# Twelve equal groups of 256 tokens, scans on full row tiles, and one listed order of jobs for all engines

## The chip, the cores and the metric

The kernel runs on one core of a Trainium2 chip. Time is device time in microseconds (us): the median of 3 runs is 389.97 us (389.54 to 390.4). The core's engines each work through their own queue in order: TensorE (PE) multiplies matrices, ScalarE (ACT) and VectorE (DVE) work element by element, GpSimd (POOL) too, and SyncE (SP) issues most transfers (DMAs). They wait for each other through semaphores.

## The reference

The input is a gated linear attention with 4 batches, 8 heads, 768 tokens and 48 features per head, followed by a channel mix.

```python
for t in range(S):
    state = alpha[:, :, t, :, None] * state + np.einsum('bhd,bhe->bhde', k[:, :, t], v[:, :, t])
    y[:, :, t] = np.einsum('bhd,bhde->bhe', q[:, :, t], state)
# x is y with the heads side by side: 384 features per token; x_prev is x one token earlier
xk = mu_k * x + (1.0 - mu_k) * x_prev
xr = mu_r * x + (1.0 - mu_r) * x_prev
k = np.maximum(xk @ w_k, 0.0)          # 384 -> 1024
v = k * k @ w_v                        # 1024 -> 384
r = 1.0 / (1.0 + np.exp(-(xr @ w_r)))  # 384 -> 384
return (r * v).astype(np.float32)
```

## The kernel before

The 768 tokens of a batch are cut into chunks of 128, and the chunks into groups: three groups of two chunks in batch 0, two groups of three chunks in each other batch, nine groups in all. The head's features lie on the partitions, two heads in one tile of 112 rows (48, a hole of 16, 48), so four such tiles (layers, `p` in the code) hold the eight heads.

Attention of a group. VectorE runs two scans per layer: a forward scan gives the running product of alpha (`pp`, line 258), a backward scan the product from a token to the group's end (`al`, line 281). q is multiplied by the one and k by the other (lines 276 and 284, on VectorE or GpSimd by the tables `QG` and `QH`). Per chunk, TensorE transposes k (`trans`, line 336, copied out by ScalarE into `ht`), and `visit` makes the state's growth (line 399), the scores (line 346), and, for the chunk before, the output from masked scores (line 365) and from the state (line 383). VectorE masks the scores (`am`, line 352), adds up the state (`st`, lines 411 and 415) and, at a group's end, rescales it (line 417). The output leaves as features on partitions (`xt`, lines 425 and 431); 16 rows of the fourth head pair's tile are moved by transfers inside SBUF into the holes of the other three (line 439), so that the channel mix sees three full tiles of 128 features.

Channel mix of a group. `mix` makes xk and xr: ScalarE scales (line 478), VectorE adds the shifted tokens (line 479); then a high part in fp32r (line 482) and the rest (line 483). `moe` multiplies high by high, low by high and high by low: `up` (line 500) 72 matmuls with the group's tokens as columns, the squares of the relu (lines 508 to 514, `kh` and `kl`), the gate (line 525) and `down` (line 540) with 384 columns. The weights come as 64-bit floats and are split into a high and a low part on the chip (`split`, lines 208 to 222), in pieces of 768 columns.

What sets the order. TensorE's and SyncE's queues follow the program text: `merge` deals the attention of group g+1 between the matmuls of group g by weights (`LEAD`, `PAD`), and in the first group `FILL` says after which of its units the weight pieces and the scans of the next groups are written. The other engines' queues are put in order by the framework's scheduler.

Of the kernel before, what the change touches and what calls it, by code (L numbers as in the profile page):

```python
# [35 lines left out]
NT = 3  # L36
NF = FF // 128
START = 2.0**30
# [4 lines left out]
LEAD = 12.0  # L43
LEAD0 = 8.0
PAD = 3.0
ENG = {
    "wk": ("AP", "AD", "AP", "AP"),
    "wr": ("DP", "DP"),
    "wv": ("DP", "DP", "AD", "DP"),
}  # L50
K2 = "AAD"
QH = ("DDDD", "PDPD", "PPPP")
QG = ("PDDD", "DPDP", "DDDP")
FILL = [
# [3 lines left out]
]  # L58
FIRST_LOADS = ["k", "wk0", "al", "wk1", "q", "wk2", "wk3", "v"]
WARM = 22  # L60
HOLD = 14
NX = HB - D

# [5 lines left out]
def merge(main, side, lead):  # L69
    total = max(sum(w for w, _ in main) - lead, 1.0)  # L70
    load = sum(w for w, _ in side)
    done = spent = 0.0
    side = list(side)
    for w, f in main:
        f()
        done += w
        while side and spent / load <= done / total:
            ws, fs = side.pop(0)
            fs()
            spent += ws  # L80
    for _, fs in side:
        fs()


@with_exitstack
def gated_attention_channel_mix(
    ctx: ExitStack,
    tc: tile.TileContext,
    al_p: bass.AP,
    q_p: bass.AP,  # L90
    k_p: bass.AP,
    v_p: bass.AP,
    mu_p: bass.AP,
    wk_p: bass.AP,
    wv_p: bass.AP,
    wr_p: bass.AP,
    q_raw: bass.AP,
    k_raw: bass.AP,
    v_raw: bass.AP,
    al_raw: bass.AP,  # L100
    out: bass.AP,
):
    nc = tc.nc
    PE, ACT, DVE, POOL = nc.tensor, nc.scalar, nc.vector, nc.gpsimd

    cp = ctx.enter_context(tc.tile_pool(name="cp", bufs=1))
    p1 = ctx.enter_context(tc.tile_pool(name="p1", bufs=1))
    p2 = ctx.enter_context(tc.tile_pool(name="p2", bufs=2))
    p3 = ctx.enter_context(tc.tile_pool(name="p3", bufs=3))
    ps = ctx.enter_context(tc.tile_pool(name="ps", bufs=1, space=PSUM))  # L110
    pm = ctx.enter_context(tc.tile_pool(name="pm", bufs=3, space=PSUM))
    dp = ctx.enter_context(tc.tile_pool(name="dp", bufs=1, space=DRAM))

    zero = cp.tile([R, R], F32, name="zero")
# [705 lines left out]
```

## Time and profile before

| | us |
|---|---|
| median of 3 runs | 389.97 |
| profiled execution, span from first to last instruction | 390.1 |
| TensorE busy | 332.0 (85%) |
| VectorE busy | 281.6 (72%) |
| ScalarE busy | 188.7 (48%) |
| GpSimd busy | 65.3 (17%) |

The profile comes from one execution; its own time is the span, with nothing to add around it that the page shows. Busy times are unions of an engine's instructions. Matmuls overlap in a pipeline, so how fast they follow each other is read from their starts, not from the length of one. PEclk is the granted share of TensorE's full clock.

### The profile page before, as it was taken

The numbers are of one execution on the slowest core, as the hardware profiler recorded it, in microseconds if no ns is written. First come the engines' busy times: TensorE is split into PE (matmuls) and PEld (weight loads), VectorE is DVE, ScalarE is ACT, GpSimd is POOL, SyncE is SP. The second block draws the span as 40 slices with busy tenths as digits, with TensorE's granted clock in tenths as the row PEclk, the third lists the DMA queues.
The fourth block names the chain that finished last, engine by engine and source line by source line (L and its number), as shares of the span: only waits on it lengthen the run. The fifth ranks groups of instructions, "written<-read, shape, count | busy, mean of one in ns | idle before, by whom it ended". The sixth has DMA issues, their size and how long they took to land.

```text
span 390.1 us, 10751 instructions
## 1 busy us (share of the span) xinstructions
PE 332.0 (85%) x4590; PEld 315.5 (81%) x4590; DVE 281.6 (72%) x513; ACT 188.7 (48%) x393; POOL 65.3 (17%) x84
## 2 busy tenths in 40 slices
PE   7542787709995997899979997999999999999993
PEld 6432687709984996799969997999999999999993
DVE  5787989998389639988596959678965476456510
ACT  3356693236563345544355525562754555455500
POOL 5143544550021003203010220003000000000000
PEclk9655769968999799999999998999999999999998
DMA  8978455830703070305510341025100110011001
GB/s 212 273 249 293 136 152 143 233 91 24 212 25 92 12 214 22 91 3 172 142 42 2 100 144 42 3 74 169 44 2 2 37 43 3 3 37 40 0 23 47
DMA packets 15958, 35.56 MB, mean 91 GB/s; under 512 B 1600, under 2 KB 9568, under 8 KB 15904
## 3 DMA queue, kind: packets, MB, share of 16 engines
q1 hardware_dynamic: 14736, 33.72, 29.2%
q10 hardware_dynamic: 1168, 1.09, 1.1%
q8 instruction: 38, 0.62, 0.7%
q14 instruction: 16, 0.13, 0.1%
HBM read 28.90 MB, written 4.72 MB: 86 GB/s over the span
## 4 chain that ended last, share of the span: by engine, by line
PE 47%; DVE 20%; DMA 6%; issue 4%; ACT 3%; ACTq 0%; DVEq 0%
PE pk L500 19%; PE pv L540 13%; PE pg L525 5%; DVE al L281 4%; DMA xt<-xt 4%; DVE pp L258 4%; DVE x L479 3%; PE yu L365 2%; DMA q<-q_p 2%; DVE xkl L483 2%; DVE q L276 1%; PE pt L336 1%; DVE kl L514 1%; PE sp L346 1%; PE yu L399 1%
## 5 line engine op out<-in xcount | busy, mean ns | idle before, releaser
L500 PE MATMUL pk<-xkh,wkh 128*128 128x384 f32 (+1 forms) x216 | 51.4, 345 | 21.7 <-ACT xkh L482 21.7
L540 PE MATMUL pv<-wvh,kl 128*128 128x384 f32 x192 | 64.9, 338 | 2.4 <-DVE kl L514 2.4
L540 PE MATMUL pv<-wvl,kh 128*128 128x384 f32 x192 | 64.7, 337 | 0.0
L540 PE MATMUL pv<-wvh,kh 128*128 128x384 f32 x192 | 64.4, 335 | 0.0
L500 PEld LDWEIGHTS pk<-xkh,wkh 128*128 128x128 f32 x216 | 37.9, 203 | 24.5 <-ACT xkh L482 23.6
L508 ACT ACTIVATE r<-pk 128x384 f32<-128x384 f32 (+1 forms) x72 | 32.3, 454 | 41.2 <-PE pk L500 38.4
L500 PE MATMUL pk<-xkh,wkl 128*128 128x384 f32 (+1 forms) x216 | 49.6, 340 | 0.0
L500 PE MATMUL pk<-xkl,wkh 128*128 128x384 f32 (+1 forms) x216 | 48.6, 335 | 0.1
L284 POOL TENSOR_TENSOR k<-k,al 112x768 f32<-112x768 f32 (+1 forms) x18 | 31.1, 1733 | 91.3 <-DVE al L281 50.0
L512 DVE TENSOR_TENSOR k<-r 128x384 f32<-128x384 f32 (+1 forms) x56 | 30.0, 535 | 22.7 <-ACT r L508 22.1
L478 ACT ACTIVATE x<-xt,mu 128x384 f32<-128x384 f32 (+1 forms) x54 | 28.5, 575 | 35.6 <-DMA xt<-xt 25.5
L514 DVE TENSOR_TENSOR kl<-k,kh 128x384 fp32r<-128x384 f32 (+1 forms) x72 | 36.7, 509 | 11.0 <-ACT kh L513 5.8
L281 DVE TENSOR_TENSOR_SCAN al<-al 112x383 f32<-112x383 f32 (+1 forms) x36 | 39.7, 1137 | 1.3 <-ACT junk L265 1.1
L500 PEld LDWEIGHTS pk<-xkl,wkh 128*128 128x128 f32 x216 | 38.4, 203 | 0.8 <-DVE xkl L483 0.3
L540 PEld LDWEIGHTS pv<-wvh,kl 128*128 128x128 f32 x192 | 36.1, 188 | 3.4 <-DVE kl L514 3.4
L500 PEld LDWEIGHTS pk<-xkh,wkl 128*128 128x128 f32 x216 | 37.2, 202 | 0.9
L258 DVE TENSOR_TENSOR_SCAN pp<-al,tiny 112x384 f32<-112x384 f32 (+1 forms) x36 | 33.9, 963 | 4.2 <-DMA al<-al_p 4.2
L540 PEld LDWEIGHTS pv<-wvl,kh 128*128 128x128 f32 x192 | 36.0, 188 | 0.0
L540 PEld LDWEIGHTS pv<-wvh,kh 128*128 128x128 f32 x192 | 36.0, 188 | 0.0
L513 ACT ACTIVATE kh<-r 128x384 fp32r<-128x384 f32 (+1 forms) x72 | 34.7, 488 | 1.4
L479 DVE SCALAR_TENSOR_TENSOR x<-xt,nu,x 128x384 f32<-128x384 f32 (+1 forms) x54 | 31.9, 631 | 2.7 <-ACT x L478 2.7
L425 ACT COPY xt<-yu 112x512 f32<-112x512 f32 x24 | 14.1, 588 | 35.8 <-DVE st L415 25.3
(149 smaller groups left out, 531.3 us busy)
## 6 DMA issues: line engine op xcount, KB each, us to landing
out<-sig SPq DMA_DIRECT2D x24, 192.0 KB, 1.9
al<-al_p SPq DMA_DIRECT2D x6, 672.0 KB, 5.3
k<-k_p SPq DMA_DIRECT2D x6, 672.0 KB, 4.7
q<-q_p SPq DMA_DIRECT2D x6, 672.0 KB, 7.4
v<-v_p SPq DMA_DIRECT2D x6, 600.0 KB, 4.2
wkraw<-wk_p SPq DMA_DIRECT2D x4, 768.0 KB, 14.6
vraw<-wv_p SPq DMA_DIRECT2D x4, 768.0 KB, 5.5
v<-v_p SPq DMA_DIRECT2D x3, 400.0 KB, 6.6
```

What stands on the lines that cost most here:

```text
L258: DVE.tensor_tensor_scan(pp[:, p], al[:, p, :n], tiny[:R].to_broadcast([R, n]), initial=START, op0=ALU.mult, op1=ALU.max,)
L281: DVE.tensor_tensor_scan(back, back, back, initial=al[:, i, n : n + 1], op0=ALU.mult, op1=ALU.bypass)
L284: (DVE if QH[min(g, 2)][p] == "D" else POOL).tensor_tensor(k[:, hp], k[:, hp], al[:, hp, 1:], op=ALU.mult)
L478: ACT.activation(x, xt[:, t, 1 : 1 + n], AF.Copy, scale=mu[:, i, t : t + 1])
L479: DVE.scalar_tensor_tensor(x, xt[:, t, 0:n], nu[:, i, t : t + 1], x, op0=ALU.mult, op1=ALU.add)
L500: PE.matmul(pk, w[:, t, cols], x[:, t], start=part == 0 and t == 0, stop=part == 2 and t == NT - 1,)
L508: ACT.activation(r, pk, AF.Relu)
L512: DVE.tensor_tensor(k2, r, r, op=ALU.mult)
L513: ACT.activation(kh[:, f], r, AF.Square)
L514: DVE.tensor_tensor(kl[:, f], k2, kh[:, f].bitcast(F32), op=ALU.subtract)
L525: PE.matmul(pg, x[:, i, cols], w[:, i], start=part == 0 and i == 0, stop=part == 2 and i == NT - 1,)
L540: PE.matmul(pv, x[:, f, cols], w[:, f], start=f == 0 and i == 0, stop=f == NF - 1 and i == 2,)
```

## The change

The kernel is rewritten. What it computes stays the same, and so do the formulas on each engine.

- Groups: all groups of the channel mix have two chunks (`N` = 256 tokens, twelve pairs `m`). The scans work on the same pairs, only the first pair is cut into two groups of one chunk.
- Row tiles: from the second pair on, the fourth layer's features are laid by the host into the holes of the other three, so scans and products work on three tiles of 128 rows. After the products, transfers inside SBUF copy the 16-row pieces into a fourth layer (`gather`, two for k and two for q in each of eleven groups), since the attention matmuls still read 48 rows per head.
- Feature tiles paired: `up` handles two blocks of 128 hidden features at once into one PSUM bank, so relu, squares and residue work on 512 columns per instruction; the high and low parts of xk and xr are made for all three tiles at once (768 columns).
- Order: every job has a name (`sf` forward scan, `sb` backward scan, `qp` and `kp` products, `gq` and `gk` gathers, `tr` transposes, `vi` visit, `mk` mask, `ad` state addition, `cx` cross addition, `mv` feature transfer, `sx` and `sy` scale and shift, `xh` and `xl` high and low part, `up`, `re`, `s2`, `sh`, `sl` the squares, `ga` gate, `dn` down, `ml` and `so` the output). `ORDER` lists all of them once, for all engines; a suffix puts a job on another engine (`:P` GpSimd, `:D` VectorE, `:A` ScalarE's DMA queue), and `#` followed by a number stands for so many dummy matmuls. `plan` only derives which jobs a job needs.
- Inputs and weights lie in DRAM as whole pieces with a contiguous run per partition; k's loads carry the empty fourth layer along.

```diff
-CUTS = [[2, 2, 2], [3, 3], [3, 3], [3, 3]]
-GROUPS = [(b, sum(cut[:i]), n) for b, cut in enumerate(CUTS) for i, n in enumerate(cut)]
+CB = S // C
+NC = B * CB
+SIZES = [[1, 1, 2, 2], [2, 2, 2], [2, 2, 2], [2, 2, 2]]
+GROUPS = [(b, sum(z[:i]), n) for b, z in enumerate(SIZES) for i, n in enumerate(z)]
 NG = len(GROUPS)
-GMAX = 3 * C
+GROUP_OF = [g for g, (_, _, n) in enumerate(GROUPS) for _ in range(n)]
...
-K2 = "AAD"
-QH = ("DDDD", "PDPD", "PPPP")
-QG = ("PDDD", "DPDP", "DDDP")
...
+PAIRED = (0,)
+LAYERS = [NP if m in PAIRED else H * D // 128 for m in HOME]
+ROWS = [R if n == NP else 128 for n in LAYERS]
+CUTS = [[slice(0, 2), slice(2, 4)] if n == NP else [slice(0, 3)] for n in LAYERS]
...
+ORDER = """
+bc.0 Lal.0 Lqq.0 Lkk.0 Lqq.1 Lal.1 Lal.2 Lvv.0 Lvv.1 jk.0.0 sf.0.0 Lkk.1 sf.0.1 Lk1 jk.0.1 sf.0.2 Lk0 rc.0.0
+sf.0.3 Lk3 sb.0.1 Lr1 qp.0.1:P qp.0.0 Lk2 rc.0.1 sb.0.0 Lqq.2 ends.0 sb.0.2 Lr0 jk.1.1 kp.0.0:P sb.0.3 Lkk.2
...
-def merge(main, side, lead):
-    total = max(sum(w for w, _ in main) - lead, 1.0)
-    load = sum(w for w, _ in side)
-    done = spent = 0.0
-    side = list(side)
-    for w, f in main:
-        f()
-        done += w
-        while side and spent / load <= done / total:
-            ws, fs = side.pop(0)
-            fs()
-            spent += ws
-    for _, fs in side:
-        fs()
...
+    def scan(g):
+        n = LAYERS[g]
+        al, kk, qq, pp = (of(x, g, n) for x in ("al", "kk", "qq", "pp"))
+        end = [f"{x}e" for x in qq]
...
+        if n < NP:
+            for j in range(2):
+                add(f"gk.{g}.{j}", "SP", lambda j=j: k.gather(g, "kk", j), kk, [*of("kk", g)[n:]] if j else [f"kk.{HOME[g]}/{SUB[g]}x"])
+                add(f"gq.{g}.{j}", "SP", lambda j=j: k.gather(g, "qq", j), qq + end, [*of("qq", g)[n:]] if j else [f"qq.{HOME[g]}/{SUB[g]}x"])
...
+    def two(self):
+        return self.POOL if self.alt == "P" else self.DVE
...
+    def forward(self, g, p):
+        n = self.group(g)[1]
+        self.DVE.tensor_tensor_scan(
+            self.get("pp", g)[:, p], self.get("al", g)[:, p, :n], self.tiny[: ROWS[g]].to_broadcast([ROWS[g], n]),
+            initial=START, op0=ALU.mult, op1=ALU.max,
+        )
...
+    def k_times(self, g, two):
+        x = self.get("kk", g)[:, two]
+        self.two.tensor_tensor(x, x, self.get("al", g)[:, two, 1:], op=ALU.mult)
+
+    def q_times(self, g, two):
+        n = self.group(g)[1]
+        x = self.get("qq", g)[:, two, :n]
+        self.two.tensor_tensor(x, x, self.get("pp", g)[:, two], op=ALU.mult)
...
+    def gather(self, g, x, j):
+        m = LAYERS[g]
+        t = self.get(x, g)
+        self.queue.dma_start(t[j * HB : j * HB + D, m], t[j * HB + D : (j + 1) * HB, :m])
...
+    def x_low(self, m, i):
+        xs = self.live[f"{('xk', 'xr')[i]}.{m}"]
+        self.two.tensor_tensor(xs[:, 1], self.live[f"x.{m}.{i}"], xs[:, 0].bitcast(F32), op=ALU.subtract)
+
+    def up(self, m, f):
+        pk = self.new(f"pk.{m}.{f}", self.slots[f"pk.{m}.{f}"], [128, 2, N], space=self.ps)
+        x = self.live[f"xk.{m}"]
+        for i in range(2):
+            for w, z in ((self.hi, 0), (self.lo, 0), (self.hi, 1)):
+                for t in range(NT):
+                    at = f * PC + t * 2 * C + i * C
+                    self.PE.matmul(
+                        pk[:, i], w["k"][:, at : at + C], x[:, z, t],
+                        start=w is self.hi and z == 0 and t == 0, stop=z == 1 and t == NT - 1,
+                    )
...
+    def square(self, m, f):
+        r = self.live[f"r.{m}.{f}"]
+        k2 = self.new(f"k2.{m}.{f}", "k2", [128, 2, N])
+        if self.alt == "D":
+            self.DVE.tensor_tensor(k2, r, r, op=ALU.mult)
+        else:
+            self.ACT.activation(k2, r, AF.Square)
...
+    def square_low(self, m, f):
+        name, j, _ = self.halves(m, f)
+        x = self.live[name][:, :, 2 * j : 2 * j + 2]
+        self.two.tensor_tensor(x[:, 1], self.live[f"k2.{m}.{f}"], x[:, 0].bitcast(F32), op=ALU.subtract)
...
+    jobs, k.slots = plan(k)
+    done = set()
+    with tc.manual_schedule():
+        k.setup()
+        for name in ORDER.split():
+            if name[0] == "#":
+                k.hot(int(name[1:]))
+                continue
+            name, _, k.alt = name.partition(":")
+            _, fn, needs = jobs[name]
+            assert needs <= done, name
+            fn()
+            done.add(name)
```

GpSimd's queue behind the first group's products and until the weights of the gate. Before (`wkl`, `wrl` low parts of weights, `q`, `k` of the second group):

```order
L222 TENSOR_TENSOR wkl<-wkraw_169,wkh 128x3x256
L289 COPY pbeg<-pp_164 112x4
L290 COPY pend<-pp_164 112x4
L292 TENSOR_SCALAR pscl<-pp_164 112x4
L276 TENSOR_TENSOR q_166<-q_166,pp_164 112x256 x2
L222 TENSOR_TENSOR wkl<-wkraw_174,wkh 128x3x256 x2
L330 COPY xt_439<-xt_209 128x3
L222 TENSOR_TENSOR wrl<-rraw_384,wrh 128x768
L284 TENSOR_TENSOR k_165<-k_165,al_163 112x256
L222 TENSOR_TENSOR wrl<-rraw_386,wrh 128x384
L284 TENSOR_TENSOR k_165<-k_165,al_163 112x256
L222 TENSOR_TENSOR wvl<-vraw_388,wvh 128x768
```

and now (`kk`, `qq` of the third and fourth group):

```order
L533 TENSOR_TENSOR wkl<-raw_k_166,wkh 128x768
L581 COPY pbeg<-pp_281 128x3
L582 COPY pend<-pp_281 128x3
L585 MEMSET qq_181 32x1
L586 TENSOR_SCALAR qq_181<-pp_281 128x3
L574 TENSOR_TENSOR qq_181<-qq_181,pp_281 128x3x256
L533 TENSOR_TENSOR wkl<-raw_k_170,wkh 128x768
L569 TENSOR_TENSOR kk_193<-kk_193,al_150 128x768
L533 TENSOR_TENSOR wkl<-raw_k_177,wkh 128x768
```

The whole products of three layers now stand in this queue between the weight subtractions, where before there were products of one layer.

VectorE's queue where the second pair's features are mixed. Before (`al`, `pp` are scans, `x`, `xkl`, `xrl` the mixed features):

```order
L281 SCALAR_TENSOR_TENSOR al_937<-al_937 112x383 x4
L545 TENSOR_TENSOR sig<-pv,sig 128x384
L276 TENSOR_TENSOR q_940<-q_940,pp_938 112x768
L479 SCALAR_TENSOR_TENSOR x<-xt_439,nu,x 128x256 x2
L276 TENSOR_TENSOR q_940<-q_940,pp_938 112x768
L483 TENSOR_TENSOR xkl<-x,xkh 128x256 x2
L258 SCALAR_TENSOR_TENSOR pp_1366<-al_1365,tiny 112x384
L479 SCALAR_TENSOR_TENSOR x<-xt_439,nu,x 128x256 x2
L545 TENSOR_TENSOR sig<-pv,sig 128x384
L483 TENSOR_TENSOR xkl<-x,xkh 128x256
L483 TENSOR_TENSOR xrl<-x,xrh 128x256
L258 SCALAR_TENSOR_TENSOR pp_1366<-al_1365,tiny 112x384 x2
```

and now (`xk` is the pair of high and low part, `al_502` the alphas of the sixth group):

```order
L757 SCALAR_TENSOR_TENSOR x_0_1047<-xt_698,nu,x_0_1047 128x256 x3
L407 CAST xk_1125<-x_0_1047 128x768
L768 TENSOR_TENSOR xk_1125<-x_0_1047,xk_1125 128x768
L840 TENSOR_TENSOR sig_0_772<-pv_0_815,sig_0_772 128x384
L757 SCALAR_TENSOR_TENSOR x_1_1121<-xt_698,nu,x_1_1121 128x256 x3
L685 TENSOR_TENSOR am_1167<-sp_1055,mask 128x512
L733 TENSOR_TENSOR xt_1025<-xt_1025,sp_1055 112x2x64 x2
L699 TENSOR_TENSOR st_112<-st_116,yu_1056 112x192
L563 SCALAR_TENSOR_TENSOR al_502<-al_502 128x255
L699 TENSOR_TENSOR st_113<-st_112,yu_1056 112x192
L563 SCALAR_TENSOR_TENSOR al_502<-al_502 128x255
```

Where six features stood one by one with their subtractions and whole scans of 384 columns between them, three shifts, one cast and one subtraction of 768 columns follow each other, with short state additions and scans of 255 columns behind.

## Rows read from the trace of the kernel before

**Rows 1.** Busy times by stage; the first line names the columns, times in us.

```profile
core 0: us, PE busy (x) PEld busy (x) DVE busy (x) ACT busy (x) POOL busy (x), PEclk, DMA share, GB/s
0.00:37.60 37.60, 18.02 (x310) 15.67 (x310) 26.77 (x47) 16.78 (x27) 15.30 (x36) 0.67 0.87 258
37.60:88.26 50.66, 32.77 (x403) 30.58 (x404) 49.60 (x76) 25.90 (x61) 24.24 (x20) 0.80 0.53 152
88.26:129.40 41.14, 36.11 (x609) 34.03 (x608) 31.12 (x61) 21.97 (x57) 5.30 (x8) 0.91 0.30 84
129.40:165.00 35.60, 31.33 (x418) 29.40 (x418) 26.44 (x51) 18.91 (x42) 5.78 (x4) 0.97 0.33 92
165.00:203.50 38.50, 35.52 (x533) 33.71 (x533) 31.78 (x59) 18.02 (x37) 5.57 (x7) 1.00 0.32 91
...
278.60:316.50 37.90, 37.90 (x569) 36.52 (x568) 24.37 (x51) 19.98 (x39) 0.19 (x1) 1.00 0.06 21
```

**Rows 2.** Chain of waits, its end: start us, duration us, engine, tile, line.

```profile
353.93 12.48 PE pk L500 x72
...
367.06 4.36 PE pg L525 x24
...
383.99 0.56 DVE sig L545
```

**Rows 3.** TensorE's timeline, first main matmuls of one pair: start us, us.

```profile
98.29 0.50 PE L500 MATMUL pk<-xkl,wkh 128*128 128x256 f32 x3
...
99.31 0.50 PE L500 MATMUL pk<-xkl,wkh 128*128 128x256 f32 x3
```

**Rows 4.** VectorE's timeline outside GpSimd's longer work: start us, us.

```profile
4.19 1.27 DVE L258 TENSOR_TENSOR_SCAN pp<-al,tiny 112x256 f32<-112x256 f32 x2 [4.19 <-DMA al<-al_p]
...
10.07 0.75 DVE L281 TENSOR_TENSOR_SCAN al<-al 112x255 f32<-112x255 f32 x1
...
16.18 0.69 DVE L352 TENSOR_TENSOR am<-sp_-1_218,mask 128x512 f32<-128x512 f32 x1 [0.21 <-PE sp_-1_218 L346]
...
24.81 0.47 DVE L431 TENSOR_TENSOR xt<-xt,sp 112x128 f32<-112x128 f32 x2
25.26 0.96 DVE L222 TENSOR_TENSOR wkl<-wkraw,wkh 128x768 fp32r<-128x768 f32 x1
26.13 0.76 DVE L276 TENSOR_TENSOR q<-q,pp 112x256 f32<-112x256 f32 x2
...
36.00 0.89 DVE L479 SCALAR_TENSOR_TENSOR x<-xt,nu,x 128x256 f32<-128x256 f32 x2 [0.18 <-ACT x L478]
...
50.12 0.55 DVE L221 CAST wvh<-vraw 128x768 fp32r<-128x768 f32 x1
...
64.83 0.34 DVE L417 TENSOR_TENSOR st<-st,pscl 112x192 f32<-112x192 f32 x1
```

**Rows 5.** Timelines of VectorE and GpSimd, three places where both work.

```profile
17.65 4.09 DVE L258 TENSOR_TENSOR_SCAN pp<-al,tiny 112x256 f32<-112x256 f32 x4
18.77 1.85 POOL L222 TENSOR_TENSOR wkl<-wkraw,wkh 128x768 fp32r<-128x768 f32 x1 [7.76 <-ACT wkh L219]
...
22.48 2.40 POOL L276 TENSOR_TENSOR q<-q,pp 112x256 f32<-112x256 f32 x2
22.62 0.80 DVE L417 TENSOR_TENSOR st<-st,pscl 112x192 f32<-112x192 f32 x1
...
179.81 4.07 DVE L281 TENSOR_TENSOR_SCAN al<-al 112x383 f32<-112x383 f32 x3
180.96 2.11 POOL L284 TENSOR_TENSOR k<-k,al 112x768 f32<-112x768 f32 x1 [13.60 <-DVE al L281]
```

**Rows 6.** Transfers of the features inside SBUF, and ScalarE's longest wait for one.

```profile
xt<-xt ACTq DMA_DIRECT2D x12, 72.0 KB, 3.7
xt<-xt ACTq DMA_DIRECT2D x4, 48.0 KB, 4.6
...
ACT x L478 <- DMA xt<-xt: 8.1, 1, 8.1
```

More of the change, by code (lines that the diff above doesn't have):

```diff
@@ new lines, with __init__, place, add @@
+class Plan:
+    def __init__(self):
+        self.jobs = {}
+        self.at = {}
+        self.last = {}
+        self.since = {}
+        self.held = {}
+        self.users = {}
+    def place(self, name, slot):
+        before = self.held.get(slot)
+        self.held[slot] = name
+        self.at[name] = (slot, before)
+        self.users[name] = []
+    def add(self, name, engine, fn, reads=(), writes=()):
+        needs = set()
+        for x in (*reads, *writes):
+            if x in self.last:
+                needs.add(self.last[x])
+            t = x.split("/")[0]
+            if t in self.users:
+                self.users[t].append(name)
+                if self.at[t][1]:
+                    needs.update(self.users[self.at[t][1]])
+        for x in writes:
+            needs.update(self.since.get(x, ()))
+            self.last[x] = name
+            self.since[x] = []
+        for x in reads:
+            self.since.setdefault(x, []).append(name)
+        needs.discard(name)
+        self.jobs[name] = (engine, fn, needs)
@@ L383, in inter @@
+        if fresh:
+            for p in range(NP):
+                for s, j in quads:
+                    rr = slice(j * HB, j * HB + D)
+                    t0 = ci * C + s * HC
                     PE.matmul(
[L384 to L389 removed]
@@ new lines, in rescale, with features, leave @@
+    def rescale(self, c):
+        g = GROUP_OF[c]
+        n = self.group(g)[1]
+        x = self.by_pair(self.before(c + 1, 0))
+        self.DVE.tensor_tensor(
+            x, x, self.get("qq", g)[:R, :, n : n + 1].to_broadcast([R, NP, D]), op=ALU.mult
+        )
+    def features(self, m):
+        name = f"xt.{m}"
+        return self.live[name] if name in self.live else self.new(name, f"xt{m % 2}", [128, NT + 1, 1 + N])
+    def leave(self, c):
+        m, h = divmod(c, CM)
+        x = self.features(m)[:R, :, 1 + h * C : 1 + (h + 1) * C]
+        self.ACT.copy(
+            x.rearrange("r i (s t) -> r i s t", s=2),
+            self.stale[c][1][:R, :, : NP * HC].rearrange("r s (i t) -> r i s t", i=NP),
+        )
@@ new lines, in gate @@
+    def gate(self, m, t):
+        pg = self.new(f"pg.{m}.{t}", self.slots[f"pg.{m}.{t}"], [128, DM], space=self.ps)
+        x = self.live[f"xr.{m}"]
+        cols = slice(t * C, (t + 1) * C)
+        for z, w in ((0, self.hi), (0, self.lo), (1, self.hi)):
+            for i in range(NT):
+                self.PE.matmul(
+                    pg, x[:, z, i, cols], w["r"][:, i * DM : (i + 1) * DM],
+                    start=z == 0 and w is self.hi and i == 0, stop=z == 1 and i == NT - 1,
+                )
@@ L577, in judge @@
-        DVE.tensor_copy(flag, pf)
-    def rows(g):
-        b, c0, _, _ = span(g)
-        at = b * S + c0 * C
-        return lambda t: out[at + t * 128 : at + (t + 1) * 128, :]
-    with tc.manual_schedule(engines={mybir.EngineType.SP}):
-        first = load(1)
-        for x in FIRST_LOADS:
-            if x[0] == "w":
-                load_wk(int(x[2]))
-            else:
-                first[x]()
-    nc.scalar.dma_start(mu, mu_p)
-    nu = cp.tile([128, 2, NT], F32, name="nu")
-    POOL.tensor_scalar(nu, mu, -1.0, 1.0, op0=ALU.mult, op1=ALU.add)
@@ new lines, in sequential @@
+                rows = self.out.rearrange("(b s) e -> b s e", b=B)
+                for t in range(CM):
+                    self.gate(m, t)
+                    self.sigmoid(m, t)
+                    for h in range(2):
+                        self.down(m, t, h)
+                    self.gated(m, t)
+                    nc.sync.dma_start(
+                        rows[ds(b, 1), m * N + t * C : m * N + (t + 1) * C, :].rearrange("o s e -> (o s) e"),
+                        self.live[f"sig.{m}.{t}"],
+                    )
```

1242 lines of the change are left out of this document (673 added, 569 removed), and 3 rows, old and new, of the table FILL.

## Prediction

> **What bounds the kernel now.** I first read the busy times by stage: the stretches are cut where a group's main matmuls begin [rows 1]. In the stretch from 278.60 us TensorE is busy for all of its 37.90 us at full clock: here only the amount of matmul work counts. In the two stretches before 88.26 us it is busy for 50.8 of 88.3 us at a granted clock of 0.67 and 0.80, while VectorE is busy for 49.60 of the 50.66 us of the second: VectorE sets the pace there. Between 88.26 and 203.50 us TensorE is idle for 5.03 + 4.27 + 2.98 = 12.3 us though VectorE is not full: waits, not amount of work.
>
> How much matmul work there is I take from the end of the chain of waits, where nothing interrupts it [rows 2]: 72 matmuls with 384 columns take 12.48 us (173.5 ns each), the same for both 72-matmul stages of a group, 24 gate matmuls 4.36 us (182 ns). With 256 columns nine start within 1.02 us (113 ns each) [rows 3]. So a group of three chunks (a chunk is 128 tokens) costs 12.48 + 27 x 0.182 + 12.48 = 29.9 us, and a pair of chunks 72 x 0.113 + 18 x 0.182 + 48 x 0.1735 = 19.8 us. The full stretch of 37.90 us holds one group of three and three chunks of attention: (37.90 - 29.9)/3 = 2.67 us per chunk. The kernel before has 6 x 29.9 + 3 x 19.8 + 24 x 2.67 = 303 us of such work in a span of 390.1 us. The tail, from the last gated product on, is 390.1 - 384.0 = 6.1 us [rows 2]. The other 81 us are lost to waits and to the low clock, some 57 of them before 88.26 us. The span and the median of the runs (389.97) agree, so the sum is made on the span.
>
> **The change part by part.**
>
> Matmul work: twelve pairs cost 12 x 19.8 + 24 x 2.67 = 301 us, so the regrouping is worth 2 us, no more. The one visit that is split in two and 24 dummy matmuls stand in front of the first main matmul, where TensorE waits for VectorE anyway.
>
> VectorE, until the second pair's first matmul. In the new order the instructions ahead of it are countable. Prices are rows outside GpSimd's work, each less the 0.09 us by which a VectorE row overlaps its successor (0.96 shown, next start after 0.87) [rows 4]. 12 forward scans of 256 columns at 0.635 and 8 of 128 at 0.36 (estimate: half and a little): 10.5 us. 10 backward scans at 0.67 and 8 short ones at 0.40: 9.9. 10 joins and 3 subtractions of 768-column weight pieces (one half as long) at 0.87: 10.9. 7 casts at 0.47: 3.3. 6 masks at 0.61: 3.7. 5 pairs of cross additions at 0.45: 2.3. 9 token shifts at 0.40: 3.6. 3 feature subtractions at 0.87: 2.6. Two products of 256 columns at 0.34, a square and a gated product: 1.8. 22 short ones (state additions, reciprocals, rescales) at the 0.34 of a rescale, since they mostly wait for each other: 7.5. Sum 56 us. From there to the first matmul of the fourth pair: 9 and 11 more scans (13.1), 15 shifts (6.0), 5 masks, 5 cross additions, 15 short ones (10.4), 3 products of 768 (2.6), 3 subtractions and casts (1.8), 8 squares, residues and gated products (4.3), another 38 us, so 94 in all. The three full row tiles take a quarter of the scans away from every group but the first two: 66 scans of 256 columns and 16 of 128 stand where 72 were, 48 of them with 384 columns.
>
> What VectorE waits for itself. Its first scan waits 4.19 us for a load [rows 4]; in the first stretch it is idle for 37.60 - 26.77 = 10.8 us in all [rows 1]. The new first tile is as large, 0.23 MB, and the scans of the next group now stand ahead of the first state addition, so I keep 4.2 and put the other waits at 5: 9.2 us.
>
> GpSimd. The order hands it more: up to the second pair's first matmul 7 weight subtractions (1.85 each, one half), 6 products of three layers (2.0), 6 small ones (1.0), 4 residues of 512 columns (1.4, between those sizes) and the small copies: 41 us; up to the fourth pair's 61 us, and 116 in the whole kernel, where the kernel before shows 15.30 + 24.24 until 88.26 us and little later [rows 1]. This work is not free, because VectorE slows while it runs [rows 5]. Four forward scans took 4.09 instead of 2.54 us beside a subtraction of 1.85: 0.84 us lost per us of GpSimd. Three backward scans took 4.07 instead of 2.76 beside a product of 2.11: 0.62. A rescale took 0.80 instead of 0.34 beside products of 2.40: 0.19. The mean is 0.55; I take 0.5, and 0.19 and 0.84 as bounds.
>
> The Trainium skill, SBUF — State Buffer, section "Who interferes with whom", says that a VectorE instruction with two SBUF inputs and a GpSimd instruction that reads SBUF exclude each other, and that the later one stands still for the whole of the other. By that rule a us of GpSimd beside a queue of scans and subtractions costs VectorE up to a us; the rows show less than that in all three places. What the kernel would take by the rule is the fourth rival below.
>
> So the second pair starts at 9.2 + 56 + 0.5 x 41 = 86 us. TensorE has 34 us of work between the two pairs' first matmuls in about 45 us; at the granted 0.80 of that stretch this is 43 us, it just fits. What is left then is 301 - 19.8 - 7 x 2.67 - 0.6 (one transpose) = 262 us, for chunks 0 to 6 have been through attention: if all of it is dense, the end is at 86 + 262 + 6.1 = 354 us. If VectorE sets the pace until the fourth pair, that one starts at 9.2 + 94 + 0.5 x 61 = 134 us, and with 222.5 us left (two pairs, the third's first stage, one gate and eleven chunks are done) the end is 362 us. The order puts about 10 us of VectorE work between the fourth pair's features and their first matmul, so VectorE can lag by that much unseen: the truth lies between, and I take the middle, 358 us. Behind the fourth pair VectorE has some 116 us of work for 222 us of matmuls; even with all of GpSimd's remaining 55 us on top it is no bound.
>
> The gathers. With three row tiles the fourth layer is copied together by transfers inside SBUF, four per group and eleven groups, behind the products and ahead of the transposes; TensorE's order is fixed, so behind a waiting transpose all main matmuls stand. The nearest transfers are those of the features: 3.7 us from issue to landing for 72 KB, 4.6 for 48 KB, and one wait of 8.1 us [rows 6]. Between the last gather and the transpose stand 4.1, 3.7, 2.1, 3.6 and 4.3 us of matmuls for groups 2 to 6, and over 15 us for all later ones. In the forecast TensorE runs behind VectorE there and the waits are hidden; without that cover they cost 5 us (at 4.6 each) to 23 us (at 8.1). Loads: whole pieces are contiguous now, and k's unused rows add some 1.4 MB; the DMA share is at most 0.33 behind 88 us [rows 1], which hides them. The feature transfers get 4 us of matmuls as cover and, from the third pair on, over 12 us more until they are used.
>
> **The rivals.** (1) GpSimd costs VectorE as little as the lowest row, 0.19: the fourth pair starts at 9.2 + 94 + 12 = 115 us, the end is at 344 us. For it speaks that many VectorE instructions read PSUM or stand idle then; against it the two higher rows. (2) The gathers stall TensorE in groups 2 to 6: 358 + 5 to 23, about 372 us. For it speaks that an order written for a short landing has no way round a late one; against it that TensorE has slack while VectorE leads. (3) The order is followed but brings nothing, since the waits of the kernel before come back in other places: 303 us of work and 81 lost, 390 us. Against it speaks that from the third pair on all features are ready over 10 us ahead. (4) Slower: GpSimd shuts VectorE out one for one until the fourth pair, 9.2 + 94 + 61 + 222.5 + 6.1 = 393 us; this decides from a cost of 0.95 us per us on. For it speaks the first row with 0.84, against it the mean of 0.55. By the Trainium skill's rule above (SBUF — State Buffer, "Who interferes with whom") this would be the likeliest outcome.
>
> **How the numbers follow.** Forecast 0.55 with 351 to 365 us, rival 1 0.15, rival 2 0.20, rival 3 0.03, rival 4 0.07. The range runs from 344 (0.19 us per us) to 383 (0.84: 9.2 + 94 + 51 + 228.6). A measurement tells 0.2% from no change: faster 0.88, same 0.03, slower 0.09.
>
> **What would show it.** In the new profile, VectorE's busy time in the first 85 us should be near 75, with GpSimd near 40; the second pair's first matmul at about 86 us and the fourth's between 124 and 134; TensorE above 95% busy from there to the end, with a busy time in the whole not far above 310; transposes waiting for gathers under 5 us in all; and a tail of about 6 us. The forecast is wrong if scans beside GpSimd take twice their clean time throughout, if idle time of TensorE ahead of transposes adds up to over 10 us, or if gaps appear behind 140 us.

## The result and the profile after

The changed kernel takes 369.5 us (median of 4 runs, 367.8 to 371.4), beside 390.2 us for the kernel before on the same chip: a ratio of 0.947, 95% interval 0.944 to 0.951. The forecast was 358 us with a range of 344 to 383: faster, as said, and 11.5 us less so than the likeliest case. The profiled run took 369.6 us, its span 367.9. Here and below medians are over all executions, ratios leave out those over 1.5% longer than the fastest of their kernel, and no trace of such a one is read.

First the busy times by stage, cut where a pair's main matmuls begin as in [rows 1]: the first pair's at 37.99 us, the second's at 82.17, the third's at 111.31, the fourth's at 128.32, the fifth's at 166.84; the last row is the ninth pair's. Columns as there. (Where the code or an expectation numbers pairs, it counts from 0: pair 4 is the fifth.)

```profile
core 0: us, PE busy (x) PEld busy (x) DVE busy (x) ACT busy (x) POOL busy (x), PEclk, DMA share, GB/s
0.00:37.99 37.99, 20.80 (x357) 19.40 (x357) 31.03 (x52) 18.98 (x34) 23.94 (x48) 0.85 0.96 351
37.99:82.17 44.18, 38.18 (x723) 36.30 (x723) 43.45 (x63) 23.45 (x42) 28.62 (x26) 0.86 0.39 115
82.17:111.31 29.14, 25.07 (x513) 23.62 (x511) 28.15 (x48) 15.60 (x30) 13.43 (x12) 0.96 0.46 137
111.31:128.32 17.01, 17.01 (x235) 16.69 (x234) 16.77 (x31) 7.12 (x14) 9.04 (x9) 0.97 0.36 104
128.32:166.84 38.52, 35.84 (x317) 35.24 (x316) 22.18 (x34) 16.99 (x33) 9.48 (x12) 0.91 0.20 63
...
268.43:298.02 29.59, 29.59 (x415) 28.96 (x413) 16.11 (x36) 13.97 (x26) 6.60 (x5) 1.00 0.06 19
```

VectorE is busy for 74.5 of the first 82.2 us and for 28.15 of the next 29.1: it still sets the pace there. The fourth pair's stage is where the surprise lies: VectorE has room (22.18 of 38.52 us), yet TensorE is idle for 2.7 us at a granted clock of 0.91. The end of the chain of waits (start, duration) answers to [rows 2]; the tail from the last gated product on is 367.9 - 361.4 = 6.5 us:

```profile
357.18 4.17 PE pv L833 x24
361.44 0.56 DVE sig L840
```

To see where time is won, I price each matmul that has started by then as the prediction does (0.113, 0.1735, 0.182 us, and 2.67 us per chunk of attention) and take the sum from the clock time. What is left is lost to waits and to the low clock, in us:

```
up to        80    100    120    140    160    200    260    end of the matmuls
before      49.4   59.1   62.5   68.2   73.3   76.7   81.0   81
after       44.7   46.3   50.9   51.1   56.7   57.0   59.2   60.1
e_four      50.5   52.4   61.6   63.0   69.5   70.6   73.5   74
e_dve4      39.7   41.6   43.6   44.6   45.2   46.1   47.8   48.8
```

The last two rows are experiments below. Of the 21 us that the change brings, 17 are won by 140 us; it then loses 5.6 us in one place, at 140 us, and 2.2 us around another, at 220 us (57.0 to 59.2), which the forecast did not have. Here is the first, in TensorE's timeline (start, us; the idle time and its releaser in brackets), with the clock around both:

```profile
140.39 0.52 PE L777 MATMUL pk<-xk,wkh 128*128 128x256 f32 x3
143.58 1.01 PE L777 MATMUL pk<-xk,wkh 128*128 128x256 f32 x3 [2.68 <-DVE sig L840]
...
221.85 0.62 PE L777 MATMUL pk<-xk,wkh 128*128 128x256 f32 x3 [1.60 <-DVE sig L840]
```

```profile
136.00:140.00 4.00, 4.00 (x28) 4.00 (x28) 3.97 (x6) 2.71 (x7) 1.54 (x2) 1.00 0.07 12
143.50:149.30 5.80, 5.72 (x24) 5.72 (x25) 3.42 (x7) 1.38 (x3) 0.00 (x0) 0.50 0.09 34
149.40:155.00 5.60, 5.60 (x38) 5.60 (x38) 0.56 (x1) 2.45 (x5) 1.30 (x1) 0.97 0.10 35
221.80:226.00 4.20, 4.15 (x35) 4.16 (x36) 1.45 (x3) 0.85 (x3) 2.50 (x6) 1.00 0.57 197
```

TensorE waits for a PSUM bank that a gated product (L840) has to leave. Behind the wait of 2.68 us it runs 5.8 us at a granted 0.50 (1.2 GHz), which doubles the price of the wait; behind the 1.60 us it stays at 1.00 (2.4 GHz). The gated product was late because VectorE was in the middle of the fifth pair's features and GpSimd slowed it there; both timelines:

```profile
134.76 1.93 DVE L768 TENSOR_TENSOR xr<-x,xr 128x768 fp32r<-128x768 f32 x1
136.62 0.68 DVE L789 TENSOR_TENSOR k<-r 128x512 f32<-128x512 f32 x1
137.22 1.91 DVE L757 SCALAR_TENSOR_TENSOR x<-xt,nu,x 128x256 f32<-128x256 f32 x2
139.17 0.56 DVE L407 CAST xk<-x 128x768 fp32r<-128x768 f32 x1
139.65 2.83 DVE L757 SCALAR_TENSOR_TENSOR x<-xt,nu,x 128x256 f32<-128x256 f32 x3
142.40 0.68 DVE L540 TENSOR_TENSOR_SCAN pp<-al,tiny 128x256 f32<-128x256 f32 x1
143.00 0.52 DVE L840 TENSOR_TENSOR sig<-pv,sig 128x384 f32<-128x384 f32 x1
```

```profile
134.47 1.41 POOL L806 TENSOR_TENSOR kh<-k,kh 128x512 fp32r<-128x512 f32 x1 [1.53 <-DVE k L789]
137.44 1.41 POOL L806 TENSOR_TENSOR kh<-k,kh 128x512 fp32r<-128x512 f32 x1 [1.56 <-DVE k L789]
139.88 1.93 POOL L768 TENSOR_TENSOR xk<-x,xk 128x768 fp32r<-128x768 f32 x1 [1.02 <-DVE xk L407]
```

A subtraction that takes 0.95 us alone takes 1.93, three shifts 2.83 instead of 1.3 (three times 0.40 plus 0.09, from the shifts of [rows 4]).

### The profile page after: what moved, and what is told of

It is laid out like the page before. It is cut to its first block, busy times and chain, and to the rows that moved or that the text cites. A ratio compares the mean times of both kernels' runs of the same rounds, so it can differ in the third digit from the quotient of the medians.

```text
span 367.9 us, 11215 instructions
## 1 busy us (share of the span) xinstructions
PE 329.2 (89%) x4854; PEld 318.9 (87%) x4854; DVE 252.7 (69%) x429; ACT 169.4 (46%) x320; POOL 129.3 (35%) x150
## 4 chain that ended last, share of the span: by engine, by line
PE 49%; DVE 29%; POOL 8%; issue 7%; ACT 4%; DMA 1%; ACTq 0%; POOLq 0%; DVEq 0%
PE pk L777 18%; PE pv L833 17%; DVE x L757 6%; PE pg L814 6%; DVE pp L540 6%; DVE al L563 4%; POOL kh L806 2%; PE yu L632 2%; PE sp L675 2%; PE yu L648 2%; DVE k L789 2%; POOL kk L569 1%; POOL wvl L533 1%; DVE xt L733 1%; PE pt L601 1%
## 5 line engine op out<-in xcount | busy, mean ns | idle before, releaser
L833 PE MATMUL pv<-wvh,kh 128*128 128x384 f32 x384 | 106.2, 344 | 0.2 <-ACT r L783 0.2
L777 PE MATMUL pk<-xk,wkh 128*128 128x256 f32 x576 | 92.1, 290 | 15.7 <-DVE xk L407 11.4
L777 PEld LDWEIGHTS pk<-xk,wkh 128*128 128x128 f32 x576 | 80.4, 197 | 16.6 <-issue 11.6
L806 POOL TENSOR_TENSOR kh<-k,kh 128x512 fp32r<-128x512 f32 x23 | 34.9, 1519 | 109.0 <-ACT k L791 46.6
L833 PEld LDWEIGHTS pv<-wvh,kh 128*128 128x128 f32 x384 | 71.1, 191 | 1.2 <-ACT r L783 0.8
L777 PE MATMUL pk<-xk,wkl 128*128 128x256 f32 x288 | 51.0, 287 | 0.0
L757 DVE SCALAR_TENSOR_TENSOR x<-xt,nu,x 128x256 f32<-128x256 f32 x72 | 42.6, 630 | 7.0 <-ACT x L751 7.0
L777 PEld LDWEIGHTS pk<-xk,wkl 128*128 128x128 f32 x288 | 42.4, 196 | 0.0
L563 DVE TENSOR_TENSOR_SCAN al<-al 128x255 f32<-128x255 f32 (+1 forms) x41 | 38.8, 979 | 2.5 <-ACT junk L554 2.2
L814 PE MATMUL pg<-wrh,xr 128*128 128x384 f32 x144 | 32.9, 342 | 0.0
L840 DVE TENSOR_TENSOR sig<-pv,sig 128x384 f32<-128x384 f32 x24 | 13.1, 550 | 21.5 <-PE pv L833 19.9
```

The lines of the kernel that those rows point to most:

```text
L563: self.DVE.tensor_tensor_scan(back, back, back, initial=al[:, p, n : n + 1], op0=ALU.mult, op1=ALU.bypass)
L757: self.DVE.scalar_tensor_tensor(x, self.live[f"xt.{m}"][:, t, :N], self.nu[:, i, t : t + 1], x, op0=ALU.mult, op1=ALU.add)
L777: self.PE.matmul(pk[:, i], w["k"][:, at : at + C], x[:, z, t], start=w is self.hi and z == 0 and t == 0, stop=z == 1 and t == NT - 1,)
L806: self.two.tensor_tensor(x[:, 1], self.live[f"k2.{m}.{f}"], x[:, 0].bitcast(F32), op=ALU.subtract)
L814: self.PE.matmul(pg, x[:, z, i, cols], w["r"][:, i * DM : (i + 1) * DM], start=z == 0 and w is self.hi and i == 0, stop=z == 1 and i == NT ...
L833: self.PE.matmul(self.live[name], x[:, z, j, cols], w["v"][:, f * DM : (f + 1) * DM], start=f == 0 and i == 0, stop=f == NF - 1 and i == 2,)
```

## The experiments

Each is the changed kernel (369.5 us, ratio 0.947) with the edit named, unless it says otherwise. Times are medians; ratios are to the kernel before, run beside them.

**e_dve: GpSimd's early work to VectorE.** In the order, the mark that sends a job to GpSimd goes from 23 jobs ahead of `up.1.0`:

```diff
-qp.0.1:P ... kp.0.0:P ... wlk0:P ... wlk3:P ... sl.0.0:P ... wlv0:P ... kp.4.0:P ... qp.4.0:P
+qp.0.1   ... kp.0.0   ... wlk0   ... wlk3   ... sl.0.0   ... wlv0   ... kp.4.0   ... qp.4.0
```

> All 23 subtractions and products that GpSimd does ahead of the second pair's first matmul are done by VectorE instead. Theory A (VectorE sets the pace there, and a us of GpSimd costs it 0.47 us, the mean of the 102 us that overlap in the changed kernel's trace): VectorE gets 15.4 us of work and is rid of 0.47 x 38.6 = 18.1 us of slowing, so the second pair starts about 3 us earlier than 82.2 us and the time is 367 (+-2) us. Rival B (price 0.19): 8 us later, 377 us. Rival C (one for one): 20 us earlier, 350 us. Rival D (GpSimd's work costs nothing and something else sets the pace): up to 15 us later, 385 us.

Measured: 363.7 us, ratio 0.933 [0.927, 0.938]. Nearest to theory A, but 1.3 us beyond its margin: the second pair starts at 77.2 us instead of 82.2, though VectorE does all the work itself. With the expectation's figures that is a price of (15.4 + 5.0)/38.6 = 0.53 us per us. GpSimd's work up to there had cost VectorE more than it took off it.

**e_casts: casts of weight pieces to ScalarE.**

```diff
-whk2:D ... whr0:D ... whv0:D ... whv1:D ... whv3:D
+whk2   ... whr0   ... whv0   ... whv1   ... whv3
```

> Five casts of weight pieces (whk2, whr0, whv0, whv1, whv3) go from VectorE to ScalarE, which is idle half of the time there. In the trace they take 2.09 + 2.04 + 0.55 + 2.10 + 0.80 = 7.6 us on VectorE, 5 x 0.47 = 2.4 us when GpSimd is quiet. Theory A (the slowing belongs to the instruction): the second pair starts 7 us earlier, time 363 us. Rival B (the slowing belongs to GpSimd's instruction, which then holds up VectorE's next one instead): only the clean 2.4 us are won, time 367 us. Rival C (ScalarE gets late): no gain or slower, 370 us or more.

Measured: 367.7 us, 0.942 [0.935, 0.949], which can't be told from the changed kernel's 0.947, and far from theory A's 363. The second pair starts at 81.7 us instead of 82.2 though 7.6 us of VectorE's rows are gone. The trace has both rivals in it. VectorE's busy time up to there falls by only 3.9 us, from 74.5 to 70.6, since other rows are longer now (rival B). And it is idle for 3.4 us more, 1.6 of them waiting for a cast that ScalarE now makes (rival C). How much of the gain each of them took is not separated.

**e_gated: two gated products earlier.**

```diff
-dn.2.0.1 gq.8.1:A ... up.3.3 ml.2.0 bc.6 sf.9.0 so.2.0
+dn.2.0.1 ml.2.0 so.2.0 gq.8.1:A ... up.3.3 bc.6 sf.9.0
-dn.5.1.1 lv.15 ... dn.5.0.1 ml.5.1 mv.7.1:A so.5.1
+dn.5.1.1 ml.5.1 so.5.1 lv.15 ... dn.5.0.1 mv.7.1:A
```

> Two gated products (pair 2's first, pair 5's second) and their stores stand earlier in VectorE's order, right behind the matmuls that they need. Theory A (the two waits of TensorE at 140.9 and 220.3 us for a PSUM bank, 2.7 and 1.6 us, and the half clock behind the first are all that is lost behind 128 us): 6 to 8 us less, 362 us. Rival B (the waits move to the next instruction of the fixed order): 2 us or less, 368 us.

Measured: 370.3 us, 0.950 [0.944, 0.956]: no gain. The two waits are gone, but TensorE now runs into the next ones, 1.7 us of the same kind at 149 us and 3.0 us at 224 us. Its waits behind 130 us (total, times, longest):

```profile
PE pt L596 <- ACT ht L601: 3.0, 1, 3.0
PE pk L772 <- DVE sig L835: 1.7, 1, 1.7
```

At 224 us ScalarE's order has the eighth pair's scaling ahead of the eviction that TensorE wants, and that scaling waits 6.98 us for a transfer of features (the longest such wait before was 8.1 us, [rows 6]). So far the wait for the bank had covered it.

**e_four: the full row tiles undone.** Four layers of 112 rows for every group, so a fourth scan each way, larger products, and no gathers; a zero tile is shared so that it fits in SBUF.

```diff
-PAIRED = (0,)
+PAIRED = tuple(range(NM))
-sf.2.2        ... sb.2.2        ... qp.2.0:P          ... gk.2.0:A ... gk.2.1:A
+sf.2.2 sf.2.3 ... sb.2.2 sb.2.3 ... qp.2.0:P qp.2.1:P ...
```

> The full row tiles are undone: every group has four layers of 112 rows, so no gathers, but a fourth forward and backward scan per group and products a third larger. Theory A (VectorE sets the pace until the fourth pair): 7 groups x 1.23 us of scans and about 3 us of larger products, less 1.1 us of waits for gathers: 10 us more, 379 us. Rival B (VectorE's extra work is hidden from the second pair on; three groups count): 5 us more, 374 us. Rival C (what the scans save, the gathers and their waits cost): same, 369 us.

Measured: 384.4 us, 0.989 [0.982, 0.996]. Theory A, and more than its 10 us: the fourth pair starts at 140.6 us instead of 128.3, and the kernel is 15 us slower. VectorE's busy time up to there is 131.6 instead of 119.4 us; of the 14.6 us by which its rows add up to more, 11.6 are scans. So with this order the row tiles carry some 15 of the 21 us. (The order was not made for four layers; a better one may exist.)

**e_twice: more VectorE work and nothing else.**

```diff
+        for _ in range(2 if 2 <= g <= 8 else 1):
             self.DVE.tensor_tensor_scan(
```

> The changed kernel with the forward scans of groups 2 to 8 done twice (same result): 21 more scans of 256 columns, 0.59 us each from start to start, 12.4 us of VectorE work ahead of the fourth pair, 5.3 of it ahead of the second. Theory A (VectorE sets the pace until the fourth pair): 12 us more, 382 us. Rival B (only until the second pair): 5 us more, 375 us. Rival C (neither; e_four's 15 us came from something else): 371 us or less.

Measured: 379.7 us, 0.974 [0.969, 0.978]: 10 us for 12.4 us of scans, theory A. The second pair starts at 88.6 us, the fourth at 139.5, 11.2 us late, with VectorE busy for 131.5 us by then, as in e_four. VectorE's amount of work up to the fourth pair is what counts, and by e_four's rows the scans are most of what the row tiles save there.

**e_pairs: the regrouping alone, in the kernel before.**

```diff
-CUTS = [[2, 2, 2], [3, 3], [3, 3], [3, 3]]
+CUTS = [[2, 2, 2], [2, 2, 2], [2, 2, 2], [2, 2, 2]]
```

> The kernel before with its groups cut to twelve pairs, nothing else. Theory A (regrouping is worth the 2 us of matmul work, the rest is order and row tiles): 388 us. Rival B (the planner's lists and leads belong to the old cut; waits come up in other places, and twelve small groups mean more VectorE work): slower, 395 us or more. Rival C (pairs begin earlier than groups of three and let the matmuls start earlier): 380 us or less.

Measured: 392.8 us, 1.005 [1.002, 1.008]: half a per cent slower, between A and B. Its trace, of the longest of its seven runs (396.8 us), is 9 us ahead at 140 us (59.3 us lost instead of 68.2) and gives that back behind 220 us. The twelve pairs are worth nothing without the new order.

**e_bench: the disputed price by itself.**

```diff
+for name, (n, fn) in kinds.items():
+    for k, two in ((0, True), (3, True), (4, False)):
+        ...  # n times fn on VectorE, beside k subtractions or copies on GpSimd
```

> The changed kernel, with a series of measurements behind it, on tiles of its own, so its time says nothing. VectorE does runs of 10 forward scans (256 columns), 14 token shifts, 12 casts of 768, 12 products of 384 with one input in PSUM, and 7 subtractions of 768; each alone, then beside 3 subtractions of 768 on GpSimd, then beside 4 copies of 768 on GpSimd. Theory A (a part of GpSimd's time only: 0.47 us per us): a run of 5.9 us of scans beside 5 us of subtractions takes 8.3 us, and so in proportion for all kinds. Theory B (whoever comes second stands still until the other has ended): the times of both engines add up, about 11 us, for scans, shifts, casts and subtractions, but the products from PSUM are not slowed. Theory C for the copies: one input on GpSimd slows VectorE as two do; or not at all.

VectorE's timeline: each kind alone, beside three subtractions, beside four copies (start, us for the whole run). The first row lacks one of its ten scans.

```profile
365.50 6.49 DVE L874 TENSOR_TENSOR_SCAN ba<-ba,tiny 128x256 f32<-128x256 f32 x9
372.02 11.61 DVE L874 TENSOR_TENSOR_SCAN ba<-ba,tiny 128x256 f32<-128x256 f32 x10
383.66 9.08 DVE L874 TENSOR_TENSOR_SCAN ba<-ba,tiny 128x256 f32<-128x256 f32 x10
...
420.93 7.11 DVE L876 CAST bb<-ba 128x768 fp32r<-128x768 f32 x12
428.06 11.68 DVE L876 CAST bb<-ba 128x768 fp32r<-128x768 f32 x12
439.78 9.22 DVE L876 CAST bb<-ba 128x768 fp32r<-128x768 f32 x12
449.04 7.07 DVE L877 TENSOR_TENSOR ba<-bps,ba 128x384 f32<-128x384 f32 x12
456.14 7.07 DVE L877 TENSOR_TENSOR ba<-bps,ba 128x384 f32<-128x384 f32 x12
```

```profile
456.38 5.57 POOL L887 TENSOR_TENSOR be<-bc,bd 128x768 f32<-128x768 f32 x3
463.46 3.47 POOL L889 COPY be<-bc 128x768 f32<-128x768 f32 x4
```

Undisturbed, a subtraction takes GpSimd 5.57/3 = 1.86 us and a copy 0.87. Three subtractions cost scans 11.61 - 7.2 = 4.4 us, shifts 4.4 (7.26 to 11.65), casts 4.6, subtractions 4.6 (6.91 to 11.49): 1.5 us each, whatever stands beside them, or 0.8 of their time. A copy costs 0.5 us. Products with an input in PSUM are not slowed at all. That is close to theory B, though not all of it: scans and subtractions take 11.6 us together, where their times alone add up to 7.2 + 5.6 = 12.8. It is a price per GpSimd instruction, which whatever instruction VectorE is at pays, unless that one reads PSUM. (The profile's spans on GpSimd are rough, so the 1.86 us are too.)

**e_dve4: GpSimd's work up to the fifth pair to VectorE.** As e_dve, for 38 jobs ahead of `up.4.0`.

> As e_dve, and also the 15 subtractions and products of GpSimd between the second and the fifth pair's first matmul go to VectorE. Theory A (VectorE sets the pace there too; a us of GpSimd costs it 0.47 to 0.56 us, the mean of the changed kernel's trace and what e_dve gave): 11.2 us of work added against 25.7 us of GpSimd x 0.47 to 0.56 = 12.1 to 14.4 us, so 1 to 3 us less than e_dve: 361 to 363 us. Rival B (behind 82 us GpSimd's work was hidden): VectorE's queue is 11 us longer, and the kernel takes 366 us or more. Rival C: no difference to e_dve, 364 us.

Measured: 357.7 us (355.3 to 359.5), 0.917 [0.911, 0.922], more than theory A's 361 to 363. Its stages, cut as above at the first five pairs:

```profile
0.00:34.95 34.95, 22.03 (x357) 20.41 (x357) 26.32 (x61) 17.25 (x31) 8.19 (x37) 0.81 0.97 342
34.95:76.92 41.97, 36.11 (x723) 34.02 (x723) 41.62 (x76) 24.93 (x46) 5.62 (x14) 0.92 0.48 154
76.92:103.22 26.30, 23.61 (x513) 22.70 (x511) 25.94 (x53) 15.66 (x30) 0.93 (x5) 1.00 0.51 151
103.22:121.23 18.01, 16.90 (x238) 16.26 (x234) 17.77 (x35) 7.53 (x16) 1.17 (x8) 1.00 0.37 102
121.23:154.70 33.47, 32.99 (x317) 32.40 (x316) 22.41 (x41) 16.44 (x31) 1.23 (x3) 1.00 0.23 71
```

The fourth pair starts at 121.2 us, and its stage, 38.5 us before, takes 33.5 at full clock with the same 22 us of VectorE. With GpSimd at 1.23 us there, the features and the gated product come in time, and the wait for the bank is 0.5 us. e_dve, which differs only in that GpSimd keeps its work between the second and the fifth pair, still has it in full. First e_dve's row:

```profile
139.67 0.62 PE L771 MATMUL pk<-xk,wkh 128*128 128x256 f32 x3 [2.75 <-DVE sig L834]
```

Then e_dve4's:

```profile
134.30 0.62 PE L771 MATMUL pk<-xk,wkh 128*128 128x256 f32 x3 [0.48 <-DVE sig L834]
```

Theory A did not count this wait. In e_dve it cost 2.75 us and some 3 us at half the clock behind it, which is about as much as e_dve4 gained beyond theory A. e_dve4 beats both kernels: 0.917/0.947 is 3% off the changed kernel.

**e_both: e_dve4 with the casts of e_casts and the first gated product of e_gated.**

> e_dve4, with the five casts of weight pieces on ScalarE as in e_casts, and the gated product and store of pair 2 early as in e_gated. Theory A (these add up: 2 us for the casts as in e_casts, 2.7 us and the half clock behind the wait at 140.9 us, 3 to 5 us): 355 to 358 us. Rival B (a wait that goes is replaced by the next one of the fixed order, as at 222 us in e_gated): 361 us or more.

Measured: 357.3 us, 0.916 [0.913, 0.920]: no different from e_dve4. That lies in theory A's range, but only because e_dve4 does too; nothing adds up. With GpSimd quiet, a cast costs VectorE only 0.5 us, and the wait that the gated product cures is already gone.

**e_best2 and e_best3: more reordering on top of e_dve4.**

```diff
 e_best2, e_best3
-sb.3.1 tr.3 sh.0.2 sc.1        sf.7.2 ... sf.7.0 ... ad.8.1        up.1.2 sc.7
+ad.1.1 sc.1                    ad.8.1 sf.7.2 sf.7.0                ad.7.1 sc.7
 e_best2                                   e_best3
-sx.7.0.1 bc.8 tr.17 ... ht.17             -gk.11.1:A ... lv.15
+tr.17 ht.17 sx.7.0.1 bc.8                 +lv.15 gk.11.1:A
```

> e_dve4 with six jobs put earlier or later in the order, so that what TensorE waits for there comes first: the gated products of pairs 2 and 5 (as in e_gated), chunk 17's transpose and its eviction ahead of pair 7's scaling on ScalarE, two rescales of the state right behind the state additions, and two scans of group 7 behind chunk 8's state additions. In e_dve4's trace TensorE stands still for 4.2, 1.5, 1.1, 0.5 and 1.5 us at these places. Theory A (the waits behind 100 us are lost time, since TensorE sets the pace there; the 4.2 us at 51 us only move, since VectorE does): 3 to 4 us less than e_dve4, 353 to 354 us. Rival B (the waits come back at the next place of the fixed order): 357 us.

> e_dve4 with jobs moved in the order once more: as e_best2, but chunk 17's transpose and eviction stay, and instead the eviction of chunk 15's result stands ahead of the gather that ScalarE issues (in e_dve4 ScalarE stands 6.7 us ahead of that eviction, since the gather waits there for GpSimd's product), and two scans of group 12 stand later. Theory A (the wait at 209 us and those behind it in e_best2 come from ScalarE's place in its own order, so this takes them away): 2 to 4 us less than e_dve4, 354 to 356 us. Rival B (a wait that goes is replaced by the next one): 358 us or more.

The edit columns above are places of the order; not shown are the two gated products of e_gated, in both runs, and two scans of group 12 in e_best3. Measured: 360.9 us (0.923 [0.919, 0.927]) and 362.3 us (0.923 [0.918, 0.929]): no gain over e_dve4's 0.917 [0.911, 0.922], rival B both times; whether they are slower the intervals leave open, since they overlap. In e_best2's trace the seventh pair starts at 208.8 us instead of 210.5, and then TensorE, being ahead, waits 2.9 us somewhere else: for ScalarE's relu, which waits for VectorE's square, which stands beside a subtraction on GpSimd and takes 2.29 us where others take 0.69. TensorE's wait (total, times, longest), then VectorE's row, GpSimd's, and the clock behind the wait:

```profile
PE pg L808 <- ACT r L777: 2.9, 1, 2.9
```

```profile
218.48 2.29 DVE L783 TENSOR_TENSOR k<-r 128x512 f32<-128x512 f32 x1
```

```profile
218.25 1.97 POOL L762 TENSOR_TENSOR xk<-x,xk 128x768 fp32r<-128x768 f32 x1 [2.44 <-DVE xk L401]
```

```profile
221.50:224.60 3.10, 3.09 (x10) 3.10 (x11) 3.03 (x7) 2.82 (x6) 0.11 (x1) 0.50 0.00 0
```

A wait of 1.5 us had been traded for one of 2.9 us, which the half clock makes dearer still. This subtraction lies behind the fifth pair, where e_dve4 leaves GpSimd its work; no run takes that work away too.

**e_gather2: each gather twice.**

```diff
+        for _ in range(2):
             self.queue.dma_start(t[j * HB : j * HB + D, m], t[j * HB + D : (j + 1) * HB, :m])
```

> The changed kernel with every gather issued twice in a row on the same queue, so that the fourth layer is there later; same data. Theory A (the gathers are hidden, TensorE waits 1.1 us for one of them in all): 370 us, at most 2 us more. Rival B (the order has no slack for them, as the prediction's second rival says): each of the gathers of groups 2 to 6 comes 2 us or more later and TensorE waits for it each time, 380 us or more.

Measured: 401.3 us, 1.025 [1.019, 1.031]. The edit did not do what I meant: the second copy writes the rows of the first and so waits for its landing, and where ScalarE issues it, all of ScalarE's instructions stand behind it. ScalarE's waits:

```profile
ACT r L779 <- DMA kk<-kk: 20.3, 3, 9.6
ACT xt L718 <- DMA qq<-qq: 17.8, 2, 14.1
```

TensorE itself waits only 4.5 us for gathers in that run. So it does not decide how well the gathers are hidden; it shows that an issue that must wait is dear on an engine that has other work.

## Why the prediction came out as it did

**VectorE's pace: right.** The forecast was 86 us for the second pair's first matmul, and 134 for the fourth's as the later end. Measured 82.2 and 128.3. VectorE was busy for 74.5 us by the first (near 75 forecast) and 119.4 by the second (94 + 0.5 x 61 = 124.5), and idle for 7.7 us by the first (9.2). Two prices were not lowered by the 0.09 us as the text says, 0.635 for a scan (1.27/2) and 0.45 for two cross additions (shown as 0.47): under 2 us in all. e_twice and e_four show that this amount of work does set the start of the fourth pair, and not only that of the second.

**The price of GpSimd: the product right, its factors off.** GpSimd was busy for 52.6 us by the second pair and 75.0 by the fourth, not 41 and 61. By the second pair its 23 listed jobs took 38.5 us, near the 35.6 that the forecast had for them; the rest is short copies, nearly twice as long as forecast, and the setting of tiles at the start, which was not counted. Over the whole changed kernel, VectorE's rows are 48.1 us longer than their undisturbed medians, over some 102 us in which GpSimd's instructions of over 0.5 us overlap them: 0.47 us per us, where the forecast had 0.5. Counted in the same way the rows are 21 us longer by the second pair and 30 by the fourth, against the forecast's 20.5 and 30.5. e_bench has 0.8 for work in SBUF and 0 for products from PSUM; in what shares the two make up the 0.47 was not measured. The last rival's one for one did not come, in no kind of instruction.

The Trainium skill, SBUF — State Buffer, section "Who interferes with whom", names the kinds: two SBUF inputs on VectorE, and copies and casts in the modes that use both ports, exclude a reading GpSimd instruction, and the one that comes second stands still for the whole of the other; one SBUF input outside those modes does not. By which kinds are slowed, e_bench agrees: scans, shifts, subtractions and casts are, products from PSUM are not. By the size it does not quite: 1.5 us of a subtraction's 1.86 are paid, not all of it.

**The rest as dense matmuls: the step that failed.** "With 222.5 us left [...] the end is 362 us" takes the matmuls from the fourth pair on as dense. From 128.3 us to the end it took 239.6 us, not 222.5 + 6.1 = 228.6. Of these 11.0 us, 5.6 are the wait at 140.9 us with the half clock behind it and 2.2 stand around the one at 220.3 us; the tail was 0.4 us longer, and 2.8 us are spread. TensorE's busy time came to 329.2 us, against "not far above 310". The prediction had named "gaps behind 140 us" as what would make it wrong. Its step "VectorE has some 116 us of work for 222 us of matmuls; even with all of GpSimd's remaining 55 us on top it is no bound" looked at amounts; the order is fixed, and one gated product behind 8 us of features was enough. e_dve4, where those features are not slowed, takes 234.4 us from the fourth pair on (e_dve 239.4): half of the miss is gone with GpSimd's work there. That the total still lies well inside the range is in part luck: the fourth pair started 5.7 us before the later end of 134 us, which hides half of the 11.0 us.

**The gathers: right, with a side effect.** TensorE waits 1.1 us for one of them, against under 5 us forecast. But a gather issued from ScalarE waits there for GpSimd's product and holds up the eviction behind it. ScalarE's timeline shows the root of the wait at 220 us:

```profile
218.47 0.58 ACTq L591 DMA_DIRECT2D kk<-kk  x1
219.09 0.59 ACT L722 COPY xt<-yu 112x512 f32<-112x512 f32 x1 [6.74 <-POOL kk L569]
```

**The regrouping: 2 us forecast, none found** (e_pairs). **The tail:** 6.5 us for 6.1. **The dummy matmuls and the paired feature tiles** were not tried by themselves.

## What to carry to other kernels

Count the bound engine's work up to the point where the next engine takes over; the full row tiles, mostly through a quarter fewer scans there, were worth 15 of the 21 us. Handing work to a neighbour that slows the bound engine needs its price first: a GpSimd subtraction of 768 columns cost VectorE 1.5 us where doing it cost 0.95. In a fixed order, a wait that you remove uncovers the next one, so follow the waits of all engines to their root before moving a job, and price a wait of TensorE with the clock behind it.

## What the runs showed of the hardware

- A GpSimd subtraction of 768 columns takes 1.5 us from VectorE's scans, shifts, casts or subtractions, a copy of 768 columns 0.5 us, and neither anything from products with one input in PSUM (7.07 us alone and beside both).
- TensorE's granted clock was 0.50 behind waits of 2.7 to 3.0 us in dense work, for some 6 us in the changed kernel (143.5 to 149.6 us) and for 3.1 to 3.2 us in e_dve, e_gated and e_best2, and 1.00 behind one of 1.6 us. Behind a wait of 2.4 us it was 0.50 for 3.0 us in the changed kernel (at 109 us) and 1.00 in e_gated (at 109.3 us), so the same wait can have two prices.
- A DMA issue that waits on ScalarE's queue stops ScalarE: 38 us of its waits in e_gather2 end with a gather's landing, and 6.74 us in the changed kernel with the product that a gather waits for.
